# RetNet recurrence and SiLU feed-forward in one kernel: the second product from unsplit float32 operands, in the four quarters of the array

## The chip, the core and the metric

The kernel runs on one core of one Trainium2 chip. Its work is done by TensorE (matrix products, with a queue for the products and one for the loads of the stationary operand, PE and PEld in the profile), VectorE (DVE), ScalarE (ACT), GpSimd (POOL) and by DMA transfers that the queue of SyncE (SP) or ScalarE issues. The metric is the device time of one execution in microseconds; lower is better. A product's accumulator is a bank of 128 partitions by 512 float32; there are eight.

## The reference

```python
# q, k, v: (4, 8, 768, 64); w_in: (512, 2048); w_out: (2048, 512)
state = np.zeros((B, H, D, D), dtype=np.float32)
for t in range(S):
    state = gamma[None, :, None, None] * state + np.einsum('bhd,bhe->bhde', k[:, :, t], v[:, :, t])
    y[:, :, t] = scale * np.einsum('bhd,bhde->bhe', q[:, :, t], state)
x = np.ascontiguousarray(y.transpose(0, 2, 1, 3)).reshape(B * S, H * D)
h = x @ w_in
g = h * (1.0 / (1.0 + np.exp(-h)))
return g @ w_out
```

All is float32. The first product is 3072 by 512 by 2048, the second 3072 by 2048 by 512: as much multiplying each.

## The kernel before

The sequence is cut into six chunks c of 128 positions (NC = 6). A unit is one chunk of one batch entry (24 units); four units of a chunk give x for 4 x 128 = 512 positions. The recurrence of a unit is computed with small float32 products of 64 rows by 64 columns, placed in the quarters of the 128 x 128 array: `stage_s` (L493) the sums of k and v over half a unit, `stage_a` (L503) the scores, `stage_y` (L544) the output. The quarter follows from the partitions: the rows from where the two operands lie, the columns from where the result goes. Where the rows differ, the result goes to another bank. `stage_t` transposes k and q on TensorE (L467, L474) up to a certain unit; later ones are transposed by DMA.

The two large products work with split operands. A float32 x is written as a rounded high part (scale HALF), a low part and a mixed third part, each stored in a type (fp32r) that TensorE takes in a single product, so that one float32 product becomes three products with full rows and columns: two into one bank (`ha`, `oa`), the third into another (`hb`, `ob`). The result is the first bank times ONE_E (1 + EPS) minus the second.

The first product, `multiply` (L703), goes over c and f: f counts the 16 blocks of 128 columns of w_in (NF = 16), and each (c, f) has 3 x 4 products of 512 positions. `close_steps` takes the banks out (ACT L713, DVE L718), applies SiLU on ACT (L723) and `put_g` stores g of (c, f), 128 x 512, to DRAM. It runs while the recurrence of later units is still going on; the two are interleaved. Its weights, three parts of each f, fill the slots `w_slot(f)` of `wpool`, of 3 x 512 a partition; the last four lie in one tile.

The second product begins when all of the first is done, because its weights take the same slots. While the last chunk of the first product goes on (`c == NC - 1` in the loop over `steps`), w_out is split: `get_w` (L750) loads the float32 block of f from DRAM to a buffer of the pools `kt` and `qt`, `w_out` (which calls `split_steps`, L121, L124, L127, L129) makes its three parts in the slot that the first product has just left; the last four are made in the first four steps of the second product. For g, `get` (L742) loads one (c, f) four ahead (G_AHEAD), and `split` (ACT L768, DVE L770 and L771) makes the three parts three ahead (S_AHEAD), in tiles of four f's. n counts (c, f) over all 96.

For each c, eight banks are accumulators: two for each of the four blocks b of 128 positions. For each f and each b three products of 128 x 128 x 512 follow (L1045): the stationary operand is a 128 x 128 piece of g, with the 128 hidden units as rows and the positions as columns, and the 512 columns of w_out's f are moved through. Behind each c the banks are taken out: `o` = `oa` times ONE_E on ACT (L1069), minus `ob` on DVE (L1070), and stored by a DMA of ACT's queue. In the last c the last two f's are put behind, block by block (L1059), so that three blocks can be taken out before the last ends, and the last block's first bank is closed in two halves of 256 columns (L1073 copies `ob` on ACT, L1078 combines on DVE, L1081 stores on SP's queue).

The order on TensorE is that of the program. On the other engines a scheduler places the instructions by their dependences, except for some that are tied to others by hand (`queue`, `issue_after`).

Of the kernel before, what the change touches and what calls it, by code (L numbers as in the profile page):

```python
# [13 lines left out]
FP32 = mybir.dt.float32  # L14
FP32R = mybir.dt.float32r
# [3 lines left out]
AF = mybir.ActivationFunctionType  # L19
ALU = mybir.AluOpType  # L20
# [8 lines left out]
EPS = 2.0 ** -12  # L29
HALF = 1.0 - 2.0 ** -13  # L30
ONE_E = 1.0 + EPS
# [3 lines left out]
def kernel(  # L35
# [28 lines left out]
    nc = tc.nc  # L64
    B, H, S, D = q.shape
    DM, DF = moe_w_in.shape
    C = 128
# [3 lines left out]
    NF = DF // 128  # L71
    NT = B * C
# [4 lines left out]
    scale = 1.0 / math.sqrt(D)  # L77
# [9 lines left out]
    xpool = pool("xpool", 2)  # L87
    const = pool("const", 1)
    ld = pool("ld", 2)
    one = pool("one", 1)  # L90
# [9 lines left out]
    wo_dram = [dram.tile([128, DM], FP32, tag=f"wo{f}", name=f"wod_{f}") for f in range(NF)]  # L100
# [7 lines left out]
    def w_slot(f, name):  # L108
        if f < NF - 4:
            return wpool.tile([128, 3, 512], FP32R, tag=f"w{f}", name=f"{name}{f}")  # L110
        if f == NF - 4:
            quads[name] = wpool.tile([128, 4, 3, 512], FP32R, tag="wq", name=f"{name}4")
        return quads[name][:, f - NF + 4]
# [18 lines left out]
    def split_w(*of):  # L132
        steps = split_steps(*of)
        next(steps)
        yield
        list(steps)
# [201 lines left out]
    for j in range(2):  # L338
        for a in range(HP):
            nc.scalar.activation(out=decay[:, j, a, :], in_=lag[:, :D], func=AF.Exp,  # L340
                                 scale=float(lg[2 * a + j]))
# [10 lines left out]
    for h in range(H):  # L352
        nc.scalar.activation(out=gk[:, 0, h : h + 1], in_=pos, func=AF.Exp,
                             scale=float(-lg[h]))
# [8 lines left out]
    for c in range(1, NC):  # L363
        nc.gpsimd.tensor_tensor(out=gk[:, c, :], in0=gk[:, c - 1, :],
                                in1=step[:, HP : HP + H], op=ALU.mult)
# [11 lines left out]
    xt, kt, qt, am = {}, {}, {}, {}  # L377
# [354 lines left out]
    order = [(c, f) for c in range(NC) for f in range(NF)]  # L732
    got, ready, wo, w_got = {}, {}, {}, {}

    def get(n):
        if n >= len(order):
            return
        c, f = order[n]
        name = "kvqkvkqv"[n % 8]
        g = ld.tile([128, NT], FP32, tag=f"{name}f", name=f"gr_{c}_{f}",  # L740
                    bufs=2 if name == "q" else 3)
        nc.sync.dma_start(out=g, in_=g_dram[c, f])  # L742
        got[n] = g

    def get_w(f):
        if f < NF:
            tag = "kqkqq"[f % 5]
            t = one.tile([128, DM], FP32, tag=f"{tag}t", name=f"wr_{f}",
                         bufs=2 if tag == "k" else 3)
            nc.sync.dma_start(out=t, in_=wo_dram[f])  # L750
            w_got[f] = t

    def w_out(f):
        list(split_w(f, w_got.pop(f), "wo", 1.0, wo))
        get_w(f + W_READ)

    blocks = {}

    def split(n):
        if n >= len(order):  # L760
            return
        c, f = order[n]
        get(n + G_AHEAD)
        g = got.pop(n)
        if f % 4 == 0:
            blocks[n // 4] = xpool.tile([128, 3, 4, NT], FP32R, tag="xt", name=f"gs_{c}_{f}")
        t = blocks[n // 4][:, :, f % 4, :]
        nc.scalar.activation(out=t[:, 0, :], in_=g, func=AF.Copy, scale=HALF)  # L768
        high = t[:, 0, :].bitcast(FP32)
        nc.vector.tensor_tensor(out=t[:, 1, :], in0=g, in1=high, op=ALU.subtract)  # L770
        nc.vector.scalar_tensor_tensor(out=t[:, 2, :], in0=t[:, 1, :].bitcast(FP32),  # L771
                                       scalar=-1.0 / EPS, in1=high,
                                       op0=ALU.mult, op1=ALU.add)
        ready[n] = t

    G_AHEAD = 4
    W_READ = 4
    S_AHEAD = 3


    sa, ys, asteps, ysteps = {}, {}, {}, {}
# [199 lines left out]
    for n, (c, f) in enumerate(steps):  # L981
        if n in scales_at:
            behind_next.append(lambda m=scales_at[n]: scale_k(m))
        if n in joins_at:
            behind_copy.insert(0, lambda m=joins_at[n]: [join_t(name, m) for name in "qk"])
        if n in parts:
            behind_next.append(lambda m=parts[n]: part_t(m, taken_out[0]))
        patient[0] = steps.index((3, 0)) <= n < max(turns_at) + 2
        product_in(c, f)
        put_g(1)  # L990
        store_w()
        if (c, f) in takes:
            take_w(taken_out[0], n < len(pairs + three))
        behind.get((c, f), lambda: None)()
        if n in turns_at:
            turn_t(turns_at[n])
            if turns_at[n] >= LATER:
                with tc.issue_after(turned_by[0]):
                    load("k", turns_at[n] + 1), load("q", turns_at[n] + 1)
        if turns_at.get(n - 1, 0) >= LATER:  # L1000
            with tc.issue_after(stored[0]):
                load("v", turns_at[n - 1] + 1)
        if turns_at.get(n - 2, 0) >= LATER:
            with tc.issue_after(stored[0]):
                while waiting:
                    load_w(waiting.pop(0))
        for name, m in loads_at.get(n, ()):
            load(name, m)
        if c == NC - 1:
            if f == 0:  # L1010
                for i in range(W_READ):
                    get_w(i)
            if f < NF - 4:
                w_out(f)
            if f >= NF - 6:
                if f == NF - 6:
                    for n in range(G_AHEAD):
                        get(n)
                if f >= NF - S_AHEAD:
                    split(f - NF + S_AHEAD)  # L1020
    put_g(0)

    for c in range(NC):
        acc = []
        for b in range(B):
            if b < 2:
                u = banks("sy"[b], f"o{b}_{c}")
                acc.append([u[:, i] for i in range(2)])
            else:
                acc.append([turn(f"oa{b}_{c}"), turn(f"ob{b}_{c}") if b == 2 else  # L1030
                            banks("q", f"ob{b}_{c}", 1)[:, 0]])
        early_f = NF if c < NC - 1 else NF - 2
        for f in range(NF):
            n = c * NF + f
            split(n + S_AHEAD)
            if n < 4:
                w_out(NF - 4 + n)
            t = ready[n]
            if f >= early_f:
                continue  # L1040
            for b in range(B):
                gh, glo, gm = (t[:, i, ts(b, C)] for i in range(3))
                oa, ob = acc[b]
                for o, g, i in (oa, gh, 0), (oa, glo, 1), (ob, gm, 2):
                    nc.tensor.matmul(o, lhsT=g, rhs=wo[f][:, i, :], start=f == 0 and i != 1,  # L1045
                                     stop=f == NF - 1 and i != 0)

        for b in range(B if early_f < NF else 0):
            oa, ob = acc[b]
            ends = [(ob, (2,), slice(None))]  # L1050
            if b < B - 1:
                ends.append((oa, (0, 1), slice(None)))
            else:
                ends += [(oa, (0, 1), slice(i * DM // 2, (i + 1) * DM // 2))
                         for i in range(2)]
            for o, parts, cols in ends:
                for f in range(early_f, NF):
                    for i in parts:
                        nc.tensor.matmul(o[:, cols], lhsT=ready[c * NF + f][:, i, ts(b, C)],  # L1059
                                         rhs=wo[f][:, i, cols], start=False,  # L1060
                                         stop=f == NF - 1 and i != 0,
                                         skip_group_check=cols.start == DM // 2)
        for b in range(B):
            oa, ob = acc[b]
            o = one.tile([128, DM], FP32, tag=("kt", "qt")[b % 2], name=f"o_{c}_{b}",
                         bufs=(2, 3)[b % 2])
            rows = ds(b * S + c * C, C)
            if c < NC - 1:
                nc.scalar.activation(out=o, in_=oa, func=AF.Copy, scale=ONE_E)  # L1069
                nc.vector.tensor_tensor(out=o, in0=o, in1=ob, op=ALU.subtract)  # L1070
                nc.scalar.dma_start(out=out[rows, :], in_=o)
                continue
            nc.scalar.copy(out=o, in_=ob)  # L1073

            n = 2 if b == B - 1 else 1
            for i in range(n):
                cols = ts(i, DM // n)
                nc.vector.scalar_tensor_tensor(out=o[:, cols], in0=oa[:, cols], scalar=ONE_E,  # L1078
                                               in1=o[:, cols], op0=ALU.mult,
                                               op1=ALU.subtract)  # L1080
                nc.sync.dma_start(out=out[rows, cols], in_=o[:, cols])  # L1081


# [28 lines left out]
```

## Time and profile before

Three runs took 618.12, 618.21 and 619.34 us, a median of 618.21. The profiled execution took 617.07 us, with a span of 615.3 us from its first to its last instruction; the granted TensorE clock was 0.999.

The span by stages, from the view that gives the busy time of each engine in chosen windows (us):

| window | what goes on | PE | DVE | ACT | PEclk | DMA share |
|---|---|---|---|---|---|---|
| 0 to 28 | recurrence alone | 23.52 | 16.61 | 18.60 | 1.00 | 0.97 |
| 28 to 300 | recurrence and first product | 269.12 | 205.67 | 198.89 | 1.00 | 0.88 |
| 300 to 349.2 | rest of the first product, split of w_out | 49.04 | 39.14 | 38.32 | 1.00 | 0.67 |
| 349.2 to 611.5 | second product | 262.29 | 133.17 | 69.13 | 1.00 | 0.33 |
| 611.5 to 615.3 | tail | 0.00 | 0.76 | 0.00 | 0.82 | 0.43 |

A busy TensorE is not one at its peak: the ends of products are modelled and overlap. How fast it works is read from the distance between the starts of products. In the lines of the profile that follow, a line of a group has the code line, the engine, the operation, the result and its operands, the shape of the array used (rows * columns) and the shape that is moved, the number of records, then busy time, mean duration in ns, and the idle time of the engine ahead of them with what ended it. A line of the timeline has the start and the length in us, then the same names and the number of records that were merged. A line of the chain has start, length, engine, result and code line.

### The profile page before, as it was taken

The numbers are of one execution on the slowest core, as the hardware profiler recorded it, in microseconds if no ns is written. First come the engines' busy times: TensorE is split into PE (matmuls) and PEld (weight loads), VectorE is DVE, ScalarE is ACT, GpSimd is POOL, SyncE is SP. The second block draws the span as 40 slices with busy tenths as digits, with TensorE's granted clock in tenths as the row PEclk, the third lists the DMA queues.
The fourth block names the chain that finished last, engine by engine and source line by source line (L and its number), as shares of the span: only waits on it lengthen the run. The fifth ranks groups of instructions, "written<-read, shape, count | busy, mean of one in ns | idle before, by whom it ended". The sixth has DMA issues, their size and how long they took to land.

```text
span 615.3 us, 13507 instructions
## 1 busy us (share of the span) xinstructions
PE 604.0 (98%) x5415; PEld 493.9 (80%) x5415; DVE 395.3 (64%) x668; ACT 324.9 (53%) x597; POOL 34.3 (6%) x90
## 2 busy tenths in 40 slices
PE   8899999999999999999999999999999999999997
PEld 5687788888887888888787888888888888888886
DVE  4788898678777676766599574635544463644631
ACT  7688778678676667667598632212221322312311
POOL 3001120100031111210000000000000000000000
PEclk9999999999999999999999999999999999999999
DMA  9999975676799799999687442523524432432301
GB/s 190 219 208 227 259 209 190 178 233 204 240 183 221 205 247 283 262 289 286 209 296 250 142 134 71 177 95 104 170 73 133 136 109 97 150 125 98 108 1 68
DMA packets 144333, 108.87 MB, mean 177 GB/s; under 512 B 101136, under 2 KB 109584, under 8 KB 144272
## 3 DMA queue, kind: packets, MB, share of 16 engines
q1 hardware_dynamic: 141392, 102.79, 60.4%
q10 hardware_dynamic: 2880, 5.24, 2.3%
q8 instruction: 42, 0.69, 0.5%
q14 instruction: 19, 0.16, 0.1%
HBM read 66.06 MB, written 36.70 MB: 167 GB/s over the span
## 4 chain that ended last, share of the span: by engine, by line
PE 93%; SPq 2%; DVE 2%; DMA 1%; ACT 1%; issue 1%; DVEq 0%; POOLq 0%
PE ha L703 29%; PE o L1045 21%; PE hb L703 14%; PE oa L1045 14%; PE ob L1045 7%; PE y L544 4%; SPq L166 2%; PE sc L493 2%; PE sc L503 1%; DMA kqv<-in_q_dram 1%; PE o L1059 0%; PE kp L467 0%; PE qp L467 0%; PE oa L1059 0%; PE kp L474 0%
## 5 line engine op out<-in xcount | busy, mean ns | idle before, releaser
L703 PE MATMUL ha<-xt,wi 128*128 128x512 f32 x768 | 193.2, 393 | 0.4 <-DVE xt L605 0.2
L703 PEld LDWEIGHTS ha<-xt,wi 128*128 128x128 f32 x768 | 142.2, 188 | 32.1 <-ACT xt L602 0.9
L1045 PE MATMUL o<-wo,gs 128*128 128x512 f32 x564 | 143.2, 389 | 0.0
L768 ACT ACTIVATE gs<-gr 128x512 fp32r<-128x512 f32 x96 | 53.7, 621 | 134.2 <-issue 131.6
L1045 PEld LDWEIGHTS o<-wo,gs 128*128 128x128 f32 x564 | 105.9, 188 | 21.9
L770 DVE TENSOR_TENSOR gs<-gr,gs 128x512 fp32r<-128x512 f32 x96 | 62.2, 686 | 90.3 <-ACT gs L768 90.3
L1045 PE MATMUL oa<-wo,gs 128*128 128x512 f32 x376 | 115.8, 389 | 0.0
L718 DVE TENSOR_TENSOR g<-g,hb 128x512 f32<-128x512 f32 x96 | 65.7, 684 | 62.8 <-ACT g L713 38.2
L703 PE MATMUL hb<-xt,wi 128*128 128x512 f32 x384 | 102.7, 389 | 0.0
L703 PEld LDWEIGHTS hb<-xt,wi 128*128 128x128 f32 x384 | 72.1, 188 | 15.1
L1045 PEld LDWEIGHTS oa<-wo,gs 128*128 128x128 f32 x376 | 70.6, 188 | 14.7
L723 ACT ACTIVATE g<-g 128x512 f32<-128x512 f32 x96 | 60.5, 630 | 38.1 <-DVE g L718 37.9
L1045 PE MATMUL ob<-wo,gs 128*128 128x512 f32 x188 | 73.7, 392 | 0.0
L713 ACT ACTIVATE g<-ha 128x512 f32<-128x512 f32 x96 | 57.0, 594 | 30.4 <-PE ha L703 20.2
L771 DVE SCALAR_TENSOR_TENSOR gs<-gs 128x512 fp32r<-128x512 f32 x96 | 62.1, 685 | 0.0
L1045 PEld LDWEIGHTS ob<-wo,gs 128*128 128x128 f32 x188 | 35.3, 188 | 8.7 <-DVE o L1070 1.6
L205 ACT ACTIVATE ca<-wf 128x512 f32<-128x512 f32 x32 | 21.6, 675 | 6.2 <-DVE cs L218 4.2
L1069 ACT ACTIVATE o<-o 128x512 f32<-128x512 f32 x10 | 6.0, 600 | 33.4 <-PE o L1045 33.0
L511 DVE TENSOR_TENSOR am<-sc,decay 128x512 f32<-128x512 f32 x24 | 16.5, 688 | 10.6 <-PE sc L503 10.5
L218 DVE SCALAR_TENSOR_TENSOR cs<-ca,cs 128x512 uint32<-128x512 uint32 x32 | 22.6, 706 | 0.9
L608 DVE SCALAR_TENSOR_TENSOR xt<-xt 128x512 fp32r<-128x512 f32 x28 | 19.9, 715 | 0.6
L544 PE MATMUL y<-qt,mid 64*64 64x64 f32 x384 | 20.0, 220 | 0.1
(113 smaller groups left out, 562.7 us busy)
## 6 DMA issues: line engine op xcount, KB each, us to landing
gd<-g SPq DMA_DIRECT2D x96, 256.0 KB, 3.6
gr<-gd SPq DMA_DIRECT2D x96, 256.0 KB, 2.7
wf<-in_moe_w_out_dram SPq DMA_DIRECT2D x16, 512.0 KB, 4.8
out_dram<-o ACTq DMA_DIRECT2D x20, 256.0 KB, 2.1
wf<-in_moe_w_in_dram SPq DMA_DIRECT2D x16, 256.0 KB, 4.5
wf<-in_moe_w_in_dram SPq DMA_DIRECT2D x32, 128.0 KB, 4.0
kf<-in_k_dram SPq DMA_DIRECT2D x16, 256.0 KB, 4.6
qf<-in_q_dram SPq DMA_DIRECT2D x16, 256.0 KB, 4.7
```

The lines of the kernel that those rows point to most:

```text
L205: top = nc.scalar.activation(out=a.bitcast(FP32), in_=hi.bitcast(FP32), func=AF.Abs, scale=2.0 ** -3).ins
L218: nc.vector.scalar_tensor_tensor(out=s, in0=a, scalar=3, in1=s, op0=ALU.logical_shift_left, op1=ALU.bitwise_xor)
L544: i = nc.tensor.matmul(yp[ts(e, D), o, a, :], lhsT=lhsT, rhs=rhs, start=(e, o) not in started, stop=True, skip_group_check=True).ins
L608: nc.vector.scalar_tensor_tensor(out=x[2], in0=x[1].bitcast(FP32), scalar=-1.0 / EPS, in1=x[0].bitcast(FP32), op0=ALU.mult, op1=ALU.add)
L703: nc.tensor.matmul(hb if i == 2 else ha, lhsT=w_sb[f][:, i, ts(kk, 128)], rhs=xt[c][:, i, kk, :], start=kk == 0 and i != 1, stop=kk == KIN ...
L713: copied[:] = [nc.scalar.activation(out=hs, in_=ha, func=AF.Copy, scale=ONE_E).ins]
L718: taken_out[:] = [nc.vector.tensor_tensor(out=hs, in0=hs, in1=hb, op=ALU.subtract).ins]
L723: nc.scalar.activation(out=hs, in_=hs, func=AF.Silu)
L768: nc.scalar.activation(out=t[:, 0, :], in_=g, func=AF.Copy, scale=HALF)
L770: nc.vector.tensor_tensor(out=t[:, 1, :], in0=g, in1=high, op=ALU.subtract)
L771: nc.vector.scalar_tensor_tensor(out=t[:, 2, :], in0=t[:, 1, :].bitcast(FP32), scalar=-1.0 / EPS, in1=high, op0=ALU.mult, op1=ALU.add)
L1045: nc.tensor.matmul(o, lhsT=g, rhs=wo[f][:, i, :], start=f == 0 and i != 1, stop=f == NF - 1 and i != 0)
```

## The change

The split of g and of w_out goes. `w_out(f)` loads the float32 block straight into the first third of the slot; `get` loads g seven n's ahead; and `product_out` multiplies pieces of 64 rows by 64 positions: for each block b, o picks the half of the block's 128 positions and r the upper or lower 64 hidden units. All four (o, r) pairs move 512 columns (256 in the last block's last two f's). r = 0 goes to the first bank of a block and r = 1 to the second, and the sum of both banks is the result, so that taking out becomes a copy on ACT and an addition on DVE. In the last c the last two f's are still behind the others, block by block, and the last block is now halved in both banks; its copies on ACT are halved too.

```diff
     def w_out(f):
-        list(split_w(f, w_got.pop(f), "wo", 1.0, wo))
-        get_w(f + W_READ)
-
-    blocks = {}
-
-    def split(n):
...
-        nc.scalar.activation(out=t[:, 0, :], in_=g, func=AF.Copy, scale=HALF)
-        high = t[:, 0, :].bitcast(FP32)
-        nc.vector.tensor_tensor(out=t[:, 1, :], in0=g, in1=high, op=ALU.subtract)
-        nc.vector.scalar_tensor_tensor(out=t[:, 2, :], in0=t[:, 1, :].bitcast(FP32),
-                                       scalar=-1.0 / EPS, in1=high,
-                                       op0=ALU.mult, op1=ALU.add)
-        ready[n] = t
-
-    G_AHEAD = 4
-    W_READ = 4
-    S_AHEAD = 3
+        wo[f] = w_slot(f, "wo")[:, 0, :].bitcast(FP32)
+        nc.sync.dma_start(out=wo[f], in_=wo_dram[f])
+
+    G_AHEAD = 7
+
+    def product_out(n, acc, blocks, cols=slice(None)):
         c, f = order[n]
+        for b in blocks:
+            for o in range(2):
+                for r in range(2):
+                    nc.tensor.matmul(acc[b][r][ts(o, D), cols],
+                                     lhsT=got[n][ts(r, D), ds(b * C + o * D, D)],
+                                     rhs=wo[f][ts(r, D), cols], start=f == 0,
+                                     stop=f == NF - 1,
+                                     skip_group_check=True)
...
-        for f in range(NF):
+        for f in range(early_f):
             n = c * NF + f
-            split(n + S_AHEAD)
+            get(n + G_AHEAD)
             if n < 4:
                 w_out(NF - 4 + n)
...
-            for b in range(B):
-                gh, glo, gm = (t[:, i, ts(b, C)] for i in range(3))
-                oa, ob = acc[b]
-                for o, g, i in (oa, gh, 0), (oa, glo, 1), (ob, gm, 2):
-                    nc.tensor.matmul(o, lhsT=g, rhs=wo[f][:, i, :], start=f == 0 and i != 1,
-                                     stop=f == NF - 1 and i != 0)
...
+            product_out(n, acc, range(B))
         for b in range(B if early_f < NF else 0):
...
+            h = 2 if b == B - 1 else 1
+            for i in range(h):
                 for f in range(early_f, NF):
+                    product_out(c * NF + f, acc, [b], ts(i, DM // h))
...
             if c < NC - 1:
-                nc.scalar.activation(out=o, in_=oa, func=AF.Copy, scale=ONE_E)
-                nc.vector.tensor_tensor(out=o, in0=o, in1=ob, op=ALU.subtract)
+                nc.scalar.copy(out=o, in_=oa)
+                nc.vector.tensor_tensor(out=o, in0=o, in1=ob, op=ALU.add)
                 nc.scalar.dma_start(out=out[rows, :], in_=o)
                 continue
-            nc.scalar.copy(out=o, in_=ob)
...
             for i in range(n):
                 cols = ts(i, DM // n)
-                nc.vector.scalar_tensor_tensor(out=o[:, cols], in0=oa[:, cols], scalar=ONE_E,
-                                               in1=o[:, cols], op0=ALU.mult,
-                                               op1=ALU.subtract)
+                nc.scalar.copy(out=o[:, cols], in_=ob[:, cols])
+                nc.vector.tensor_tensor(out=o[:, cols], in0=o[:, cols], in1=oa[:, cols],
+                                        op=ALU.add)
                 nc.sync.dma_start(out=out[rows, cols], in_=o[:, cols])
```

More of the change, by code (lines that the diff above doesn't have):

```diff
@@ L743, in get @@
         got[n] = g
[L745 to L751, printed above, removed]
-    def w_out(f):
-        list(split_w(f, w_got.pop(f), "wo", 1.0, wo))
-        get_w(f + W_READ)
-    blocks = {}
-    def split(n):
-        if n >= len(order):
-            return
-        c, f = order[n]
[L763 to L768, printed above, removed]
-        high = t[:, 0, :].bitcast(FP32)
-        nc.vector.tensor_tensor(out=t[:, 1, :], in0=g, in1=high, op=ALU.subtract)
-        nc.vector.scalar_tensor_tensor(out=t[:, 2, :], in0=t[:, 1, :].bitcast(FP32),
-                                       scalar=-1.0 / EPS, in1=high,
-                                       op0=ALU.mult, op1=ALU.add)
-        ready[n] = t
-    G_AHEAD = 4
-    W_READ = 4
-    S_AHEAD = 3
+    def w_out(f):
+        wo[f] = w_slot(f, "wo")[:, 0, :].bitcast(FP32)
+        nc.sync.dma_start(out=wo[f], in_=wo_dram[f])
+    G_AHEAD = 7
+    def product_out(n, acc, blocks, cols=slice(None)):
+        c, f = order[n]
+        for b in blocks:
[6 more added lines that the diff above has]
+                                     skip_group_check=True)
     sa, ys, asteps, ysteps = {}, {}, {}, {}
@@ L1009 @@
         if c == NC - 1:
-            if f == 0:
-                for i in range(W_READ):
-                    get_w(i)
             if f < NF - 4:
                 w_out(f)
[L1015 to L1020, printed above, removed]
+            if f == NF - 6:
+                for n in range(G_AHEAD):
+                    get(n)
     put_g(0)
@@ L1032 @@
         early_f = NF if c < NC - 1 else NF - 2
-        for f in range(NF):
+        for f in range(early_f):
             n = c * NF + f
-            split(n + S_AHEAD)
+            get(n + G_AHEAD)
             if n < 4:
                 w_out(NF - 4 + n)
-            t = ready[n]
-            if f >= early_f:
-                continue
-            for b in range(B):
-                gh, glo, gm = (t[:, i, ts(b, C)] for i in range(3))
-                oa, ob = acc[b]
-                for o, g, i in (oa, gh, 0), (oa, glo, 1), (ob, gm, 2):
-                    nc.tensor.matmul(o, lhsT=g, rhs=wo[f][:, i, :], start=f == 0 and i != 1,
-                                     stop=f == NF - 1 and i != 0)
-        for b in range(B if early_f < NF else 0):
[L1049 to L1056, printed above, removed]
-                for f in range(early_f, NF):
[L1058 to L1062, printed above, removed]
+            product_out(n, acc, range(B))
+        for b in range(B if early_f < NF else 0):
+            h = 2 if b == B - 1 else 1
+            for i in range(h):
+                for f in range(early_f, NF):
+                    product_out(c * NF + f, acc, [b], ts(i, DM // h))
         for b in range(B):
```

## The prediction

> **What bounds the kernel now.** I read the shares of the chain first, then TensorE's granted clock, then the groups of the second product.
>
> ```profile
> span 615.3 us, 13507 instructions
> ...
> PEclk9999999999999999999999999999999999999999
> ...
> PE 93%; SPq 2%; DVE 2%; DMA 1%; ACT 1%; issue 1%; DVEq 0%; POOLq 0%
> ...
> L768 ACT ACTIVATE gs<-gr 128x512 fp32r<-128x512 f32 x96 | 53.7, 621 | 134.2 <-issue 131.6
> ...
> L770 DVE TENSOR_TENSOR gs<-gr,gs 128x512 fp32r<-128x512 f32 x96 | 62.2, 686 | 90.3 <-ACT gs L768 90.3
> ```
>
> TensorE is 93% of the chain, at full clock, while ScalarE and VectorE, which split g in three (L768, L770, L771), sit idle 134.2 and 90.3 us before that work. Splitting is covered; what TensorE streams is paid. The table of the five windows ahead of this text puts the second product at 349.20 to 611.50 us. The chain in order of time gives its cadence:
>
> ```profile
> 349.37 1.36 PE o L1045 x6
> 352.08 1.36 PE o L1045 x6
> 354.81 1.36 PE o L1045 x6
> ```
>
> One n (one c and f) has 12 products (4 blocks by 3 parts) and takes 2.72 us: 0.2267 us a product of 512 columns. 96 n's are 261.2 us. With waits of about 0.2 us at each of five changes of c (the group of weight loads on L1045 names VectorE's L1070, 1.6 us in all) the stage streams for 262.1 us.
>
> **The price of a float32 product, which this change puts in place of three split ones.** The trace has no float32 product of 512 columns; it has the recurrence's, 64 rows by 64 columns in the same four quarters, 64 columns moved. L503 has 16 calls a unit and 24 units, 384 calls, and 768 records: one call is two records. How fast they follow is seen by cutting the timeline at three places:
>
> ```profile
> 13.35 0.24 PE L503 MATMUL sc<-qt,kt 64*64 64x64 f32 x4
> ...
> 13.35 0.30 PE L503 MATMUL sc<-qt,kt 64*64 64x64 f32 x8
> ...
> 13.35 0.59 PE L503 MATMUL sc<-qt,kt 64*64 64x64 f32 x28
> ```
>
> The first four start within 0.02 us (0.24 less one record's 0.22), four quarters at once. Each further four add (0.59 - 0.24)/6 = 0.058 us. So in one quarter a record of 64 columns takes 58 ns, and four quarters run beside one another. What a column costs comes from the transposes, float32 too, one record a call, and from the tail's half-wide split products:
>
> ```profile
> 11.88 0.60 PE L467 MATMUL qp<-ident,kqv 128*128 128x128 f32 x4
> ...
> 57.79 0.22 PE L474 MATMUL kp<-ident,kf 64*128 64x64 f32 x1
> ...
> 57.85 0.22 PE L474 MATMUL kp<-ident,kf 64*128 64x64 f32 x1
> ...
> 610.38 1.11 PE L1059 MATMUL oa<-wo,gs 128*128 128x256 f32 x8
> ```
>
> Transposes of 128 columns follow every (0.60 - 0.27)/3 = 0.110 us (0.27 is the last one's own length, the group's mean of 272 ns), those of 64 every 0.06: about 0.8 ns a column. Split products: (1.11 - 0.28)/7 = 0.119 us at 256 columns against 0.2267 at 512, 0.42 ns a column. So float32 streams a column in twice the time of a split operand, and a call makes two such records: four units of streaming where the split makes three.
>
> A record of 512 columns by these rows: 58 + 448 columns x 0.84 (twice 0.42) = 434 ns. Ends of the price: 58 + 448 x 0.8 = 416 ns below, 8 x 58 = 464 ns above (the fixed part growing with the columns). I take 433, nearest to the first, since its columns are as many. A call is 2 x 433 = 866 ns, four calls (o and r) run in the four quarters at once, and there are 96 n's by 4 blocks: 384 x 0.866 = 332.5 us (319.5 to 356.4).
>
> The Trainium skill, "FP8 and Floating Point Precision", section TensorE Precision Notes, says that a true float32 product makes four passes through the array (high and low of either operand). By that alone the stage would take 4/3 of 261.2, 348.3 us, and the whole some 704 us; the rows give less because the quarters' records carry a smaller fixed part than the split products do.
>
> **The other parts.**
> - Split of g: 96 ACT (621 ns) and 192 DVE (686, 685 ns) gone, 59.6 and 131.7 us. All lay beside TensorE: nothing. Were g late, its load would show it: seven of eight buffers are in flight, 7 x 3.46 = 24 us ahead of a load that lands in 2.7 us; without that cover 2.7 us once.
> - Split of w_out (L121, L124, L127, L129, 16 times): gone from the last chunk of the first product and four n's. The timeline there shows one place where TensorE waited for VectorE's L718 behind it, at 335.47 us, cadence gaps of some 0.43 us in sum. I take -0.4 (0 to -0.5).
> - w_out's loads go straight into the weight slots: still 16 of 256 KB on SP. Each waits until the first product of the same f has read the slot, and what stands behind it on SP is the store of the g just made and w_out's own stores; these wait for work after that same product anyway. The last four wait for the end of the first product; eight g's are loaded ahead of them, and row 12 is needed 12 x 3.46 = 41 us later. Nothing; if uncovered, one 2.7 us landing.
> - Change of c: a block's banks are emptied by a 0.60 us copy and a 0.69 us add, now begun 2.6 us (three blocks) before the end for block 0; the last has 2.6 us before its next turn. The five waits of 0.2 us may go; 262.1 already holds them.
> - Tail: the last half needs a 256-column ACT copy behind the last product, which was done ahead before. The full one takes 0.59, so an estimate of 0.35 us; but VectorE was held 0.43 us there by the half before (two L1078 in 0.76). I take +0.1 (0 to +0.5).
>
> Sum: -262.1 + 332.5 - 0.4 + 0.1 = +70.1 us. On the profiled execution, span 615.3 and 617.07 in all, that is 687.2; the median of the runs, 618.21, is 1.1 higher: **688.3 us**. Own range 675 to 713 by the ends of the price.
>
> **Rivals.**
> *Faster: the second unit of streaming isn't there.* Read alone, 58 ns at 64 columns could be mostly fixed: at 0.42 ns a column 27 ns stream and 31 are the load of the quarter's weights. A record of 512 is then 31 + 215 = 246 ns, the stage 768 x 0.246 = 189 us, the whole 545 us. It decides for not slower from a record of 262.1/768 = 341 ns down. For it: weight loads of 64 columns fill the same rounds. Against it: the transposes' 0.8 ns a column, and 64-column transposes load 128 columns of weights in a 60 ns round, so a load of half as many can hardly fill 58.
>
> *Much slower: the quarters don't stay apart on long streams,* since both records of a call go to one quarter and follow each other in the program. If products start strictly in program order, the next quarter begins only with the second record of the last; two quarters at most are busy, and a call costs one record's time: 1536 x 0.433 = 665 us, the whole 1021 us. Two streams of the same rows in each other's way would cost as much. Against it, from the timeline:
>
> ```profile
> 16.73 0.23 PE L544 MATMUL y<-qt,mid 64*64 64x64 f32 x2
> 16.75 0.27 PE L493 MATMUL sc<-kqv 64*64 64x64 f32 x2
> 16.79 0.28 PE L544 MATMUL y<-qt,mid 64*64 64x64 f32 x4
> ```
>
> Those four calls of y stand ahead of the sc calls in the program and use the upper rows alone; two sc records start in the lower rows before the second records of y. And y's two quarters, which share their rows, take the same 0.06 us a round as L503's four. Shown for 64 columns only.
> The Trainium skill, "TensorE: Matmul & The Clock Gate", Part 3, The mechanism, states the rule behind this rival: products start and end strictly in program order, only weight loads are pulled ahead. These rows disagree with it.
>
> *Slower than forecast: the fixed part grows with the columns,* 464 ns a record: 618.2 + 356.4 - 262.4 = 712 us. For it only that no row excludes it; against it 0.119 and 0.2267, whose fixed part is the same 12 ns at both widths.
>
> That the change doesn't take place has no room: every call of the second product is written anew.
>
> **How the numbers follow.** Forecast 85%; faster rival 5%; apart-failing rival 5%; growing fixed part 5%. The likeliest gives 688. The range of 8 in 10 is 682 to 706: its lower end is a record of 425 ns, its upper one of 456; it leaves out the three rivals and some 5% of the forecast's own. Faster than by 0.2% needs the first rival: 5%. Within 0.2%, 1.2 us, about what this measurement can tell from none, needs a record at 341 ns by chance: 1%. Slower: 94%.
>
> **What would show it.** The records of the second product's line: 3072 of 64x512, starting in fours, a round every 0.43 us; 3.46 us for one n; TensorE never waiting for DMA or VectorE between 349 and 682 us, and the stage 332 us long; ACT and DVE all but idle in it; the gap at 335 us gone; a tail within half a microsecond of 3.8. Rounds of 0.25 us, or records in pairs, would make the forecast wrong, and so would a granted clock that falls in a stage that has nothing but quarter products: the recurrence alone, the first 28 us, kept it at 1.00.

## The result and the profile after

The changed kernel took 690.38 us (median of four runs, 689.61 to 691.54) against 618.78 us before (618.12 to 620.93): a ratio of 1.1152, 95% interval 1.1119 to 1.1185. It is slower, as forecast, by 71.6 us; forecast were 70.1 and 688.3 us.

The page of the changed kernel answers the lines shown of before: span, granted clock in 40 slices, shares of the chain, and the groups of the second product, now on L756.

```profile
span 689.8 us, 16916 instructions
...
PEclk9899999999999999999999999999999999999999
...
PE 95%; SPq 2%; DMA 2%; DVE 1%; issue 1%; ACT 0%; DVEq 0%; POOLq 0%
...
L756 PE MATMUL oa<-wo,gr 64*64 64x512 f32 (+1 forms) x776 | 238.0, 585 | 0.0
L756 PE MATMUL o<-wo,gr 64*64 64x512 f32 x1536 | 237.8, 589 | 0.0
...
L756 PE MATMUL ob<-wo,gr 64*64 64x512 f32 (+1 forms) x776 | 181.5, 585 | 0.0
```

TensorE is still nearly all of the chain. L768 and L770 have left the list, and the second product is 3088 records (1536 + 776 + 776; 1156 before). Two windows of the profile after (window, its length, busy time of PE, PEld, DVE, ACT and POOL with their records, granted clock, DMA share, GB/s) answer the table of before:

```profile
0.00:28.00 28.00, 22.17 (x502) 14.58 (x504) 16.87 (x32) 17.92 (x46) 5.44 (x45) 0.96 0.99 201
...
349.20:686.00 336.80, 336.42 (x3099) 190.44 (x3097) 16.51 (x25) 15.18 (x28) 0.00 (x0) 1.00 0.31 92
```

VectorE and ScalarE lost 117 and 54 us of work in that stage and nothing came of it; TensorE streams longer. This profiled execution (691.54 us) also lost 2.7 us in the recurrence's early part, its first 65 us, where its clock fell (0.96 over the first 28 us, 1.00 in the profile of before). The change has no edit there, so this is no part of it.

From the first record of the second product to the start of its last, 349.203 to 611.208 us before and 351.516 to 685.241 after, it went from 262.0 to 333.7 us: +71.7. The gap at 335 us in the first product is gone: -0.45. From the last start to the end of the span 4.06 became 4.53: +0.47. Sum +71.7, and the medians differ by 71.6.

The cadence, read as before from merged records at the beginning of the stage:

```profile
351.52 0.66 PE L756 MATMUL o<-wo,gr 64*64 64x512 f32 x4
...
351.52 1.95 PE L756 MATMUL o<-wo,gr 64*64 64x512 f32 x16
```

Four records start at once; twelve more, three rounds, take (1.95 - 0.66)/3 = 0.43 us each. From one record to the fourth behind it 429 ns are the commonest distance in the whole stage. The four start together up to the first change of c; from there on nearly always three start together and one some 0.13 us apart from them, at the same pace.

Below, "a chunk" is the distance between the first records of two successive values of c in the second product. It is a better measure of that stage than whole times, which differ by some 2 us between executions.

| kernel | chunk, us (first; later ones) | time, us |
|---|---|---|
| before | 43.52; 43.71 to 43.73 | 618.78 |
| changed | 54.98; 55.41 to 55.78 | 690.38 |
| e1, whole array | 54.93; 54.93 | 685.35 |
| e2, row halves | 55.04; 55.53 to 55.90 | 690.14 |
| e3, by quarter | 115.06; 115.42 to 115.83 | 1042.6 |
| e4, high halves | 15.70; 17.70 to 19.31 | 464.96 |
| e5, split operands in row halves | 43.68; 45.05 to 45.25 | 625.55 |
| e7, store from SP's queue | 54.98; 54.93 | 686.54 |
| e8, pairs of blocks | 55.01; 56.04 to 56.10 | 693.67 |

e1 to e4 and e8 are one run each; beside e1 to e4 the kernel before took 623.02 us in its one run, beside e8 618.09.

### The profile page after: what moved, and what is told of

It is laid out like the page before. It is cut to its first block, busy times and chain, and to the rows that moved or that the text cites. A ratio compares the mean times of both kernels' runs of the same rounds, so it can differ in the third digit from the quotient of the medians.

```text
span 689.8 us, 16916 instructions
## 1 busy us (share of the span) xinstructions
PE 676.8 (98%) x7347; PEld 467.9 (68%) x7347; DVE 259.5 (38%) x444; ACT 256.7 (37%) x470; POOL 33.6 (5%) x90
## 4 chain that ended last, share of the span: by engine, by line
PE 95%; SPq 2%; DMA 2%; DVE 1%; issue 1%; ACT 0%; DVEq 0%; POOLq 0%
PE ha L703 26%; PE o L756 24%; PE ob L756 14%; PE hb L703 12%; PE oa L756 10%; PE y L544 3%; PE sc L493 2%; PE sc L503 1%; DMA kqv<-in_k_dram 1%; SPq L166 1%; DMA kqv<-in_v_dram 1%; PE kp L467 1%; SPq L188 1%; PE qp L467 0%; PE kp L474 0%
## 5 line engine op out<-in xcount | busy, mean ns | idle before, releaser
L756 PE MATMUL oa<-wo,gr 64*64 64x512 f32 (+1 forms) x776 | 238.0, 585 | 0.0
L756 PE MATMUL o<-wo,gr 64*64 64x512 f32 x1536 | 237.8, 589 | 0.0
L756 PE MATMUL ob<-wo,gr 64*64 64x512 f32 (+1 forms) x776 | 181.5, 585 | 0.0
L756 PEld LDWEIGHTS o<-wo,gr 64*64 64x64 f32 x1536 | 95.7, 133 | 71.5 <-issue 67.3
L756 PEld LDWEIGHTS oa<-wo,gr 64*64 64x64 f32 x776 | 93.1, 133 | 21.7 <-issue 17.7
L1027 DVE TENSOR_TENSOR o<-o,o 128x512 f32<-128x512 f32 x10 | 6.9, 688 | 261.7 <-ACT o L1026 261.7
L1026 ACT COPY o<-o 128x512 f32<-128x512 f32 x10 | 5.9, 586 | 261.7 <-PE o L756 256.0
L718 DVE TENSOR_TENSOR g<-g,hb 128x512 f32<-128x512 f32 x96 | 65.8, 685 | 81.7 <-PE hb L703 42.1
L756 PEld LDWEIGHTS ob<-wo,gr 64*64 64x64 f32 x776 | 56.3, 133 | 52.0 <-issue 47.7
L1034 DVE TENSOR_TENSOR o<-o,o 128x512 f32<-128x512 f32 x2 | 1.4, 689 | 49.5 <-ACT o L1033 49.5
L1033 ACT COPY o<-o 128x512 f32<-128x512 f32 x2 | 1.2, 586 | 49.8 <-PE o L756 49.8
```

What stands on the lines that cost most here:

```text
L718: taken_out[:] = [nc.vector.tensor_tensor(out=hs, in0=hs, in1=hb, op=ALU.subtract).ins]
L756: nc.tensor.matmul(acc[b][r][ts(o, D), cols], lhsT=got[n][ts(r, D), ds(b * C + o * D, D)], rhs=wo[f][ts(r, D), cols], start=f == 0, stop=f ...
L1027: nc.vector.tensor_tensor(out=o, in0=o, in1=ob, op=ALU.add)
```

## The experiments

**The array not cut (e1) and cut in halves (e2).**

```diff
-            for o in range(2):
-                for r in range(2):
-                    nc.tensor.matmul(acc[b][r][ts(o, D), cols],
-                                     lhsT=got[n][ts(r, D), ds(b * C + o * D, D)],
-                                     rhs=wo[f][ts(r, D), cols], start=f == 0,
...
+            # e1
+            nc.tensor.matmul(acc[b][f % 2][:, cols], lhsT=got[n][:, ts(b, C)],
+                             rhs=wo[f][:, cols], start=f < 2, stop=f >= NF - 2,
...
+            # e2
+            for r in range(2):
+                nc.tensor.matmul(acc[b][r][:, cols], lhsT=got[n][ts(r, D), ts(b, C)],
+                                 rhs=wo[f][ts(r, D), cols], start=f == 0,
...
```

> The changed kernel with its float32 products unsplit and uncut: one call of 128 rows by 128 positions in place of four of 64 by 64, even f to a block's first bank and odd f to its second. Theory (the cost is four units of streaming 512 columns, however the array is cut): a call makes two records of 427 ns of streaming and 3 to 13 ns beside, so 859 to 880 ns a block, a stage of 330 to 338 us and 690 to 699 us in all. Rival (the quarters are what costs, a whole-array float32 product would be cheaper): under 300 us for the stage, under 660 in all. Rival (the quarters save much): 15 us or more above the changed kernel's 690.

> The changed kernel with products of 64 rows by 128 positions, two halves of the array in place of four quarters. Theory: the same streaming in each half, rounds of two records every 429 ns, 690 us within 2. If two streams that share their rows were in each other's way in the quarters, this would be faster than 690 by more than 5 us.

e1 took 685.35 us and its stage 329.4 us: the stage is at the lower end of the theory's 330, the whole time 5 us below its 690, and both are far from either rival. Its timeline has single records in place of fours:

```profile
399.48 1.88 PE L754 MATMUL oa<-wo,gr 128*128 128x512 f32 x4
401.19 1.88 PE L754 MATMUL o<-wo,gr 128*128 128x512 f32 x4
```

Four records in 401.19 - 399.48 = 1.71 us, 0.43 each, the same as a round of four quarter records, and one whole-array record does as much as four. e2 took 690.14 us; the rate is the same again. So the price is that of the float32 product, and the cut neither costs nor saves streaming. What I had not expected is that e1 is 5 us faster than the changed kernel: its chunks are all 54.93 us, 128 records of 429.2 ns, while the changed kernel's later ones are up to 0.85 longer. That became the question of e7.

**Float32 against one narrow operand type (e4).**

```diff
-                                     lhsT=got[n][ts(r, D), ds(b * C + o * D, D)],
-                                     rhs=wo[f][ts(r, D), cols], start=f == 0,
+                                     lhsT=top(got[n])[ts(r, D), ds(b * C + o * D, D)],
+                                     rhs=top(wo[f])[ts(r, D), cols], start=f == 0,
...
+    def top(t):
+        return t.bitcast(BF16).rearrange("p (c w) -> p w c", w=2)[:, 1]
```

> The changed kernel with the upper two bytes of each float32 read as bfloat16, the lower two left out: quarters, order, loads and taking out as they are, and one narrow operand type in place of float32. Theory (float32 costs two records of two units each): one record a call, a round of four every 216 to 227 ns, a quarter of the changed kernel's streaming: 83 to 87 us for the stage where neither the load of g (256 KB for one n in 0.9 us) nor the taking out (some 5 us at each change of c) ends last; with these 440 to 475 us in all. Rival (a record's cost in a quarter is mostly its own start and weight load): rounds well above 300 ns.

464.96 us, a stage of 106.4 us. Two rounds of the trace:

```profile
354.72 0.39 PE L759 MATMUL ob<-wo,gr 64*64 64x512 bf16 x1
354.72 0.39 PE L759 MATMUL oa<-wo,gr 64*64 64x512 bf16 x1
...
354.94 0.39 PE L759 MATMUL ob<-wo,gr 64*64 64x512 bf16 x1
354.95 0.39 PE L759 MATMUL oa<-wo,gr 64*64 64x512 bf16 x1
```

A round takes 226 to 227 ns and a call is one record (1544 in all), where float32 makes two of 429: 858 against 227 ns a call, 3.8 to 1. 384 rounds of 227 ns are 87 us; the rest of the 106 are waits, at each change of c above all (a chunk of 16 x 4 x 0.227 = 14.5 us takes 17.7). The two chunks of 19.3 us hold a stretch in which the granted clock fell (0.91 over each of them, 1.00 over the others, with rounds of up to 427 ns), so that part of the stage is the clock. The rival, records mostly made of their own start and weight load, is out: it asked for rounds well above 300 ns.

**The order of the quarters (e3, e8).**

```diff
-        for b in blocks:
-            for o in range(2):
-                for r in range(2):
+        # e3; e8 takes the blocks two at a time in this order
+        for o in range(2):
+            for r in range(2):
+                for b in blocks:
```

> The changed kernel with the loop over the four blocks inside that over the quarters: eight records for one quarter follow each other in the program before the next quarter's turn. If each quarter is fed from what stands ready in TensorE's queue, however far behind in the program, up to some depth: 690 to 700 us, records still in fours. If products start in program order, one quarter works at a time but at the seams: 8 x 0.429 us for each quarter, some 14 us for one n, over 1500 us in all. A depth that holds less than the 32 records of one n shows as something between.

> The changed kernel with two blocks in a row for each quarter: four records for one quarter stand together in the program, where the run with all four blocks had eight and worked two quarters at a time. Theory (about four records for a quarter are held while it is busy, and the program stands still at the fifth): four are held, the other quarters' records are reached, all quarters work, 429 ns a round of four and 688 to 696 us in all. Rival (anything but an alternation from call to call halves the work): stage near 660 us, 1020 to 1050 us in all. Rival (two records are held): the stage twice as long too.

e3: 1042.6 us, a stage of 685.3. `o` is blocks 0 and 1, `oa` and `ob` the two banks of blocks 2 and 3:

```profile
352.81 0.59 PE L756 MATMUL oa<-wo,gr 64*64 64x512 f32 x1
352.82 0.64 PE L756 MATMUL o<-wo,gr 64*64 64x512 f32 x1
353.24 0.59 PE L756 MATMUL oa<-wo,gr 64*64 64x512 f32 x1
353.30 0.59 PE L756 MATMUL o<-wo,gr 64*64 64x512 f32 x1
```

Records start in pairs every 0.43 to 0.49 us, the last four of one quarter (blocks 2 and 3) beside the first four of the next (blocks 0 and 1). Neither answer I had written down alone is right, but the one in between is: the next quarter begins when the one ahead has about four records left. e8, with runs of four records, works all quarters: 693.67 us, its first chunk 55.01 us. The later chunks lose 1.1 us at the changes of c, more than the changed kernel. So about four records are held for a busy quarter, and the fifth stops whatever stands behind it in the program. That it is a queue for each quarter fits all of this but is argued, not shown.

**The waits at a change of c (e7).** In the changed kernel's timeline at the first change, VectorE, ScalarE with its DMA issues, and TensorE, taken from three views:

```profile
406.60 0.69 DVE L1027 TENSOR_TENSOR o<-o,o 128x512 f32<-128x512 f32 x1 [1.07 <-ACT o L1026]
408.32 1.29 DVE L1027 TENSOR_TENSOR o<-o,ob 128x512 f32<-128x512 f32 x2 [1.03 <-ACT o L1026]
```

```profile
405.98 0.59 ACT L1026 COPY o<-o 128x512 f32<-128x512 f32 x1 [1.17 <-PE ob L756]
407.32 0.34 ACTq L1028 DMA_DIRECT2D out_dram<-o  x1
407.70 1.07 ACT L1026 COPY o<-oa 128x512 f32<-128x512 f32 x2 [1.13 <-DVE o L1027]
```

```profile
408.34 1.07 PE L756 MATMUL oa<-wo,gr 64*64 64x512 f32 x2
409.06 0.64 PE L756 MATMUL ob<-wo,gr 64*64 64x512 f32 x1
```

Block 1 is copied at 405.98, added at 406.60, stored at 407.32, and only then does ScalarE copy block 2, at 407.70: its queue had stood at the store, which waits for the add. From copy to copy that is 1.72 us, twice what the quarters take for a block (0.86). Block 2's second bank is asked for at 408.34 and has its records at 409.06, behind the add that ends at 409.00.

```diff
-                nc.scalar.dma_start(out=out[rows, :], in_=o)
+                nc.sync.dma_start(out=out[rows, :], in_=o)
```

> The changed kernel with the stores of the first five chunks' results issued from SP's queue and not from ACT's. Theory: at each change of c ACT's queue waits for VectorE's add before it can issue a block's store, and only then copies the next block, 1.7 us a block against the 0.86 us in which the quarters ask for the next one; so a change of c costs 0.85 us (a chunk takes 55.78 us against 54.93 without any wait). With the store elsewhere a block costs VectorE's 0.69 us, every bank is free in time, a chunk takes 54.93 to 55.0 us, and the whole about 4 us less than the changed kernel: 686 us. Rival (the 0.85 us belong to both banks being begun anew in the quarters, or to quarters that fall out of step): a chunk stays at 55.8 us, 690 us.

686.54 us (four runs, 685.69 to 687.46), ratio to the kernel before 1.1096, interval 1.1049 to 1.1144; chunks of 54.93 us, a stage of 329.5. All 772 rounds have four records, and only one, the first, is longer than 430 ns. In e7's timeline the copies follow one another while TensorE goes on:

```profile
404.25 0.58 ACT L1026 COPY o<-o 128x512 f32<-128x512 f32 x1 [0.22 <-PE o L756]
...
405.10 0.58 ACT L1026 COPY o<-oa 128x512 f32<-128x512 f32 x1 [0.26 <-PE ob L756]
...
405.71 0.69 DVE L1027 TENSOR_TENSOR o<-o,ob 128x512 f32<-128x512 f32 x1 [0.16 <-ACT o L1026]
...
405.95 0.58 ACT L1026 COPY o<-oa 128x512 f32<-128x512 f32 x1 [0.27 <-PE ob L756]
```

0.85 us from copy to copy, the pace of the products. The theory holds. The rival's first half, a cost of beginning both banks anew, falls: e7 begins them anew too. Its second half, quarters out of step, is there in the changed kernel from the first change of c on, but within a chunk the pace stays at 429 ns, and in e7 it is gone together with the waits.

e1 keeps its stores on ScalarE's queue and still waits at no change of c. In its timeline three copies stand ahead of the first store, where the changed kernel has one:

```profile
402.31 0.58 ACT L1022 COPY o<-o 128x512 f32<-128x512 f32 x1 [51.01 <-PE o L754]
402.79 0.59 ACT L1022 COPY o<-oa 128x512 f32<-128x512 f32 x1
403.27 0.60 ACT L1022 COPY o<-o 128x512 f32<-128x512 f32 x1
403.65 0.37 ACTq L1024 DMA_DIRECT2D out_dram<-o  x1
```

With even and odd f in different banks, a first bank is also complete one f earlier and a second bank asked for one f later. Which of these spares e1 the wait was not tested apart.

**The split operands in row halves (e5).** Two widths in one trace give what a record carries beside its streaming. A float32 record follows the one ahead every 429.2 ns at 512 columns and every 215.9 at 256 (e1 and e7, last block): 213.3 ns for 256 columns, so 426.6 of streaming and 2.6 beside. A split product takes 226.7 and 120 ns (kernel before): 213.4 of streaming and some 13 beside. Whether the cut into parts of the array takes these 13 ns away is the question.

```diff
-                for o, g, i in (oa, gh, 0), (oa, glo, 1), (ob, gm, 2):
-                    nc.tensor.matmul(o, lhsT=g, rhs=wo[f][:, i, :], start=f == 0 and i != 1,
-                                     stop=f == NF - 1 and i != 0)
+                for g, i in (gh, 0), (glo, 1), (gm, 2):
+                    for r in range(2):
+                        nc.tensor.matmul(acc[b][r], lhsT=g[ts(r, D)],
+                                         rhs=wo[f][ts(r, D), i, :], start=f == 0 and i == 0,
...
+        if name == "wo":
+            nc.scalar.activation(out=w[:, 2, :], in_=lo, func=AF.Copy, scale=-1.0 / ONE_E)
```

> The kernel before with its three split products cut into two row halves of 64 by 128, the upper rows into one bank and the lower into the other; the sign and scale of the third product go into w_out's third part (one more ACT instruction for each f), so that both banks hold the same sum. Question: the fixed 13 ns beside 213 ns of streaming that a whole-array split product pays (0.2267 us for 512 columns) against 3 ns in the quarters of the changed kernel (0.429 us for 1024). If the row cut takes it away: rounds of 216 ns, 1152 x 10.7 ns = 12 us off the second product, some 606 us, ratio 0.98. If it belongs to the split operand's type: rounds of 227 ns and 618 us, ratio 1.00 within 0.3%. If two halves cannot stream side by side in this type: twice the stage, 880 us.

625.55 us, ratio 1.0129, interval 1.0107 to 1.0151. The halves do stream side by side, but a round still takes 226 to 227 ns: the row cut doesn't remove the 13 ns. The chunks grew by 1.3 to 1.5 us: ScalarE's copies of blocks 0 and 1 begin at 391.17 and 392.94 us with the store of block 0 at 392.52 between them, the wait of the changed kernel again (e2 has it too: copies at 403.31 and 405.06, the store at 404.64). Both banks of a block are also asked for at once, as in the changed kernel; the two weren't tested apart here.

**Is the split of g free? (e6, e9)**

```diff
+    seen = const.tile([128, 1], FP32, tag="seen", name="seen")
...
         g = got.pop(n)
+        if n >= 4:
+            ready[n] = ready[n % 4]
+            nc.vector.tensor_copy(out=seen, in_=g[:, :1])   # e9: nc.gpsimd
+            return
```

> The kernel before with g split for the first four n alone; all later n multiply those four's parts again (their g is loaded, one column of it is read, and its split is left out). TensorE's work is as before. Theory (the split of g lies wholly beside TensorE, so taking it away gains nothing): 618 us, ratio 1.00 within 0.3%. Rival (the split holds TensorE up at places, and its end is part of what the change gives back): faster by over 2 us, ratio under 0.996.

> As the run without the split of g (all n from the fifth on multiply the first four's parts, their own split is left out), but the one column of each g is read by GpSimd and not by VectorE, whose queue stood waiting for those loads in the last steps of the first product. Theory (the split of g lies beside TensorE): a second product of 262 us as before, a first product of its old length, 618 us, ratio 1.00 within 0.3%. Rival (the split holds TensorE up): ratio under 0.996.

By the whole times neither theory: 623.77 us (ratio 1.0123, 1.0081 to 1.0166) and 626.26 us (1.0128, 1.0079 to 1.0178). By stages the second product took 262.3 and 262.2 us from first to last start, against 262.0; the loss lies ahead of it (3.8 us in e6's profile, 12.5 in e9's). The waits of e9 between 300 and 360 us (who waited for whom: us in total, times, longest):

```profile
POOL seen L768 <- DMA gr<-gd: 57.1, 24, 9.2
...
PE y L544 <- POOL token L400: 4.9, 1, 4.9
```

The one-column read that I had put in waited for its load in GpSimd's queue, ahead of a small instruction that TensorE waits for in the recurrence. This wait of 4.9 us is part of the 12.5 only: 5.1 were lost before 290 us, where the clock of that execution fell too (0.94 in the first 28 us), and it fell again from 300 to 312 us (0.87). In e6 VectorE waited 13.2 us for the same loads between 300 and 360 us, and TensorE's weight loads waited 3.1 us there for L718 (0.6 before). So the second product gains nothing by the split's removal, which is what the prediction used; the whole times don't test the split, since they carry the read that I put in.

## Why the prediction was right, step by step

- *Two records a call, twice the time a column, four quarters at once.* All three hold. The record was priced at 433 ns and takes 429.2; its lower and upper ends were 416 and 464. The error has two parts. A split product of 256 columns was read as 119 ns, the mean of seven distances, of which the first is 113; the last five are 120 ns, and with these a float32 column costs 0.833 ns in place of 0.84, 3 ns less over 448 columns. And a round of 64 columns, 58 ns, has some 5 ns beside 53 of streaming, where a record of 512 has 2.6. In all 768 x 3.8 ns = 2.9 us too much. The smaller fixed part that keeps the stage under 4/3 of the old one is there, but it isn't the quarters': e1 has it on the whole array.
- *The change of c.* This is the step that failed. It said that a block's banks are emptied by a copy of 0.60 and an add of 0.69 us begun 2.6 us before the end, and that the five waits of 0.2 us may go. They grew to 0.85 us each, 4.3 us in all: the sum left out that ScalarE's queue also issues the store, which waits for the add, so that a block costs 1.72 us and not 0.7. Before, the scheduler had set three copies ahead of the first store; the sum put the new kernel's waits at nothing without asking what stands in ScalarE's queue. So TensorE did wait for VectorE within the stage (its weight loads up to 0.7 us at a time for the add L1027), where the prediction expected that it never would.
- The two errors, 2.9 us too much and 4.3 too little, partly cancel: 332.5 us were forecast for the stage and 333.7 measured, of which 329.4 to 329.5 (e1, e7) are streaming. That the sum came within 1.5 us of the measured 71.6 is luck to this extent; the price of a record, which decides for slower, is not.
- *The gap at 335 us:* -0.4 forecast, -0.45 measured. That it came from w_out's split on VectorE is read from the timeline of before; no run takes this split away alone.
- *The tail:* +0.1 forecast, 0 to +0.5 bounded, +0.47 measured. The prediction let the last half's copy run while VectorE was held by the half before. But the first half's copy, 0.37 us, began only at 685.67 us, behind the last products of both halves (last start 685.24), so that it lies wholly ahead of the two adds, whose distance of 0.34 us is the same as before.
- *Splitting is covered:* the stage's own length in e6 and e9 bears it out.
- *The loads* stayed hidden: TensorE's weight loads waited 0.6 us for g in the whole stage.
- *The faster rival* needed a record of 246 ns; e4 shows what one unit costs, 227 ns, and a float32 record takes two, 429 ns.
- *The rival of quarters that don't stay apart* had the right price for the wrong condition: 1021 us by strict order, and e3 took 1042.6 where eight records for one quarter stand together. Strict order would have given e3 over 1500 us, and in the changed kernel the first records of all four quarters start before any second one. By the Trainium skill, "TensorE: Matmul & The Clock Gate", Part 3, The mechanism, products start strictly in program order; these runs disagree.
- *The rival of a fixed part that grows with the columns* falls: 2.6 ns at 512 columns, about 5 at 64.

## What to carry to other kernels

A whole float32 product costs four units of streaming here (858 ns a block of 512 columns), a product split in three costs three (680 ns), and cutting full 128 x 128 operands into quarters changes neither: first count what TensorE streams, since work saved beside it is worth nothing while TensorE is the chain. Where several tiles of the array are to work at once, alternate them from call to call; eight records in a row for one quarter halved the rate. When banks are handed back by a chain over two engines, include every DMA that the first engine issues in between: a store that waits on the second engine ties the next block's copy to it.

## What had not been expected of the hardware

In these runs the time beside the streaming goes with the record's kind and not with how the array is cut: 13 ns for one unit of 213 (split operands on the whole array 226.7, in row halves 226 to 227; bfloat16 in quarters takes as long), but 2.6 ns for a float32 record of two units (429.2 on the whole array as in quarters). And TensorE reached the next quarter's records past about four held ones of a busy quarter, not past eight.
